# Router products of two tiles at once: 256 columns in odd steps of an attention loop, their sums over chunks in even steps

## The chip, the cores and the metric

The kernel runs on one core of one Trainium2 chip. The metric is the device time of one execution in microseconds. The trace comes from one profiled execution, whose times count from its first instruction.

## The reference

Attention within chunks of 64 rows is followed by a mixture of experts with one expert per token, all in fp32. In short:

```python
# q, k, v: (8, 8, 576, 64); chunks of 64 along the sequence
scores = q_c @ k_c.T / 8
attn = softmax(scores)
x = (attn @ v_c) -> (4608, 512)          # tokens x (heads * head_dim)

g_logits = x @ w_group                   # 4 groups
g_idx, g_w = argmax, its softmax weight
e_logits = x @ w_expert[g_idx]           # 4 experts of the group
e_idx, e_w = argmax, its softmax weight
y = relu(x @ w1[g, e]) @ w2[g, e]        # 512 -> 1024 -> 512
out = g_w * e_w * y
```

The router is the two products of x with w_group and with all four w_expert, 4 + 16 = 20 columns in all.

## The kernel before

**Tiles and stages.** The 4608 tokens are 36 tiles of 128, and 4 tiles make a routing group (groups 0 to 8). A tile passes through stages that a loop runs in steps, each stage on another tile, so that a step t works on up to six tiles. The order of the instructions of TensorE, VectorE and ScalarE is the order of the program, written out by hand (the `run` strings of the loop at L659 to L673, EXTRA, and TAIL for what comes behind). Step t issues:

- `b(t+1)`, stage_b, L294: scores of a tile, 16 small matmuls of 64x64 array tiles, into `scb[(t+1) % 2]`, a pair of PSUM banks. The scores fill columns 0 to 255 of either bank.
- `n(t-3)`, stage_norm, L339: VectorE takes the denominators (L343), their reciprocals (L345), one tile's row positions (L530, for the scatter of x to HBM on GpSimd's queue), and multiplies (L354) into x.
- `s(t)`, stage_sub, L304: VectorE takes the row maximum (L308) and subtracts it (L312).
- `c(t-1)`, stage_ct, L320: TensorE transposes the probabilities (L324), ScalarE copies them out of PSUM (L326).
- `tile_e(t)`, L378, from step 4 to step 32: the router, below.
- `p(t-2)`, stage_pv, L329: probabilities times values (L336), into the one pair of banks `ob`.
- four steps of routing (`more(4)`) on VectorE, then `e(t)`, the exponential on ScalarE (L318).
- `x(t-3)`, stage_xt, L359: TensorE transposes x (L366), ScalarE copies it to `xT` (L367), which holds the four tiles of a group.
- loads of q, k and v on SyncE's queue, and every fourth step `stage_e3` (L474), which ranks a group's tokens.

**The router.** The 512 channels of x are four chunks of 128. With tau = t - 4, `tile_e` multiplies tile tau by the 20 router columns (padded to 32) chunk by chunk: four matmuls (L387), each with a 128x32 weight `wg[:, c]` and 128 columns of `xT`, each in its own 32 columns of the array, so that they stand side by side on 128 partitions of PSUM, one chunk under the other. These are not summed in PSUM. The sum over the chunks, which also turns tokens onto partitions, is a matmul of its own (L391): the copied products of the tile before, 128x128, are its weights, and the constant `C_SEL`, 128x20, adds the four chunks. One copy of ScalarE (L392) brings both out of PSUM, 148 columns: the products of tile tau and the logits of tile tau - 1, into a slot of `lt8`. Both lie in columns 256 to 403 of the second bank of `scb[(t+1) % 2]`. After the logits of a group's last tile, at t = 4g + 8, `tile_e` queues `route(g)` (L412), whose steps VectorE takes whenever `more` is called: maximum (L421), comparison (L426), difference (L428), the first index (L432), then the softmax weights.

The last two groups, 7 and 8, don't go through `tile_e`: `stage_e1` (L369) multiplies a whole group's 512 columns at once and `stage_e2` (L398) sums its four tiles with four matmuls, in TAIL.

**Instructions.** One fp32 matmul of the program stands in the trace as two weight loads (PEld) and two matmuls (PE), the transposes as one of each. A step's scores, for instance, are 32 and 32.

**Beside the loop.** In steps 24 to 31 the first expert is prepared: GpSimd loads its weights, ScalarE casts them (L217), GpSimd subtracts (L218). Behind the loop and TAIL comes the expert part (from L731), two thirds of the time, which the change doesn't touch.

Of the kernel before, what the change touches and what calls it, by code (L numbers as in the profile page):

```python
# [9 lines left out]
F32 = mybir.dt.float32  # L10
# [9 lines left out]
P = 128  # L20
B, H, SEQ, HD = 8, 8, 576, 64
CH = 64
# [7 lines left out]
NG = 4  # L30
RPE = N // P
NG0 = NT // NG
GL = NG0 - 1
# [20 lines left out]
for _n in range(3 * NV, 3 * B):  # L54
# [3 lines left out]
C_ID, C_TRI, C_SEL, C_BASE, C_IOTA4, C_TID, C_T17, C_I64, C_J128, C_FORCE, C_BE, C_PBASE, C_E, C_PM, C_I16, C_PJ, C_PQ, C_PMIN, C_PNEED, C_N = (  # L58
    0, 128, 256, 276, 292, 296, 332, 349, 413, 449, 450, 451, 452, 453, 455, 471, 473, 475, 476, 477)
# [54 lines left out]
def moe_kernel(tc, qk, v, wgs, w1, w2, cst, out):  # L114
    nc = tc.nc
    w1 = w1.rearrange("g e d f -> (g e) d f")
    w2 = w2.rearrange("g e f d -> (g e) f d")
    with ExitStack() as ctx:
# [5 lines left out]
        cs = wpool.tile([P, C_N], F32, name="cs")  # L124
# [95 lines left out]
        with ExitStack() as c1:  # L220
            cpool = c1.enter_context(tc.tile_pool(name="cp", bufs=1))
# [7 lines left out]
            scb = [ps_s.tile([P, 2, 512], F32, name="sc%d" % i) for i in range(2)]  # L229
# [3 lines left out]
            def bank():  # L233

                ring.append(ring.pop(0))
                return ring[-1]
# [16 lines left out]
            wg = cpool.tile([P, 4, 32], F32, name="wg")  # L253
# [5 lines left out]

            xbufs = [cpool.tile([P, NG, XW], F32, name="x%d" % i) for i in range(3)]  # L260

            lt8 = cpool.tile([P, 2 * NG, P + 20], F32, name="lt8")

            st, TL = {}, NT - 1

# [103 lines left out]
            def stage_e1(g):  # L369
                xT = st["xT", g]  # L370
                lt = bank()
                for c in range(4):
                    nc.tensor.matmul(lt[32 * c:32 * c + 32, :], lhsT=wg[:, c, :], rhs=xT[:, c, :], start=True, stop=True)
                lts = lt8.rearrange("p a b -> p (a b)")[:, 0:512]
                nc.scalar.copy(lts, lt)
                st["lts", g] = lts

            def tile_e(t):  # L378

                n = (GL - 1) * NG  # L380
                e = scb[(t + 1) % 2][:, 1, 4 * CH:4 * CH + P + 20]
                t -= 4
                lo, hi = (0 if t < n else P), (P + 20 if t else P)
                if lo == 0:
                    g, i = divmod(t, NG)
                    for c in range(4):
                        nc.tensor.matmul(e[32 * c:32 * c + 32, 0:P], lhsT=wg[:, c, :], rhs=st["xT", g][:, c, i * P:i * P + P],  # L387
                                         start=True, stop=True)
                t -= 1
                if t >= 0:  # L390
                    nc.tensor.matmul(e[:, P:P + 20], lhsT=lt8[:, (t - 1) % 8, 0:P], rhs=cs[:, C_SEL:C_SEL + 20], start=True, stop=True)  # L391
                nc.scalar.copy(lt8[:, t % 8, lo:hi], e[:, lo:hi])  # L392
                if last(t):
                    g = t // NG
                    st["lg", g] = lt8[:, g % 2 * NG:g % 2 * NG + NG, P:P + 20]
                    routing.append(route(g))

            def stage_e2(g):  # L398
                lts = st["lts", g]
# [208 lines left out]
            routing = []  # L608
# [19 lines left out]
            def last(t):  # L628
                return t >= 0 and t % NG == NG - 1
# [8 lines left out]
            def run(seq):  # L638
                g = dict(u=warm_up, P=prep_static, X=first_x, L=first_l1, H=first_hi, D=first_lo, W=prep2_hi, w=prep2_lo, y=lambda i: prep2_lo(i, nc.vector), F=first_loads, R=reload, V=load_v,
                         Q=load_qk, q=load_first, I=load_cs, G=load_wg, C=casts, B=banks, Z=prefill)  # L640
                f = dict(b=stage_b, s=stage_sub, c=stage_ct, e=stage_exp, p=stage_pv, n=stage_norm, x=stage_xt)
                for z in seq.split():
                    if z[0] == "m":
                        more(int(z[1:]))
                    elif z[0] in g:
                        g[z[0]](int(z[1:]))
                    elif z[0] == "1":
                        stage_e1(int(z[1:]))
                    elif z[0] == "2":
                        stage_e2(int(z[1:]))  # L650
                    elif z[0] == "3":
                        stage_e3(int(z[1:]))
                    elif 0 <= int(z[1:]) < NT:
                        f[z[0]](int(z[1:]))

            with tc.manual_schedule(engines={mybir.EngineType.PE, mybir.EngineType.DVE, mybir.EngineType.Activation}):
                run(HEAD)
                run("u8 b0 u6")
                for t in range(TL - 2):  # L659
                    run("b%d n%d s%d c%d" % (t + 1, t - 3, t, t - 1) if t > 2 else ("b1 s0", "c0 b2 s1", "p0 b3 s2 c1")[t])  # L660
                    if 4 <= t <= 4 + (GL - 1) * NG:
                        tile_e(t)
                    run("p%d" % (t - 2) if t > 2 else "")
                    more(4)
                    run("e%d" % t)
                    stage_ex()
                    if t % 2 and t // 2 + NQ < NT // 2:
                        run("Q%d" % (t // 2 + NQ))
                    run("x%d" % (t - 3))
                    run(" ".join("V%d" % n for n in VS.get(t, ())))  # L670
                    if last(t - 7):
                        run("3%d" % ((t - 7) // NG))
                    run(EXTRA.get(t, ""))  # L673
                run(TAIL)
                assert not waiting
# [11 lines left out]
        def ft(n, name):  # L687

            at[0] += n
            return w2r[1].rearrange("p a b -> p (a b)")[0:E1, at[0] - n:at[0]]  # L690

        col = lambda c, n=1: cs[0:E1, c:c + n]
        co, a, na, s4, thr, end = ft(2, "co"), ft(RPE, "a"), ft(2, "na"), ft(4, "s4"), ft(1, "thr"), ft(1, "end")
# [732 lines left out]
```

## Time and profile before

| | us |
|---|---|
| three timed runs | 622.61, 632.97, 638.04 |
| their median | 632.97 |
| the profiled execution | 624.93 |
| its span, first to last instruction | 623.3 |
| mean granted TensorE clock of the span | 0.975 |

The page of the profile gives each engine's busy time and the share of the span. The chain of waits is the work that ended last, followed back from the end. The timeline merges instructions of one line that follow one another; "x8" is their number, and a bracket is the time for which the engine sat idle ahead of them, with what ended it ("issue" is nothing that the profile shows). [...] PE is TensorE's matmuls, PEld its weight loads, DVE is VectorE, ACT ScalarE, POOL GpSimd.

### The profile page before, as it was taken

What the parts mean: (1) busy time and instruction counts of PE and PEld (TensorE: products, weight loads), DVE (VectorE), ACT (ScalarE), POOL (GpSimd) and SP (SyncE); (2) the same over time, 40 slices, a digit from 0 to 9 for tenths busy, and PEclk for the clock granted to TensorE, in tenths of its full rate; (3) what the DMA queues carried; (4) which work ended last, traced back from release to release, by engine and by line L of the source; (5) the groups of instructions that cost most, each with busy time, mean ns of one, the idle gap of its engine ahead of it and who ended that gap; (6) DMA issues with size and microseconds to landing.
All of it is one profiled execution on the core that took longest, in us unless ns stands there. A gap on an engine that the chain in (4) does not pass through costs nothing.

```text
span 623.3 us, 16433 instructions
## 1 busy us (share of the span) xinstructions
PE 585.0 (94%) x5823; PEld 504.8 (81%) x5824; DVE 366.4 (59%) x688; ACT 264.9 (43%) x368; POOL 152.9 (25%) x279
## 2 busy tenths in 40 slices
PE   6889899966799999989999999999999999999995
PEld 3667677754789899878889899989989988898984
DVE  4577769885678682127497674735425578854311
ACT  2455556644246361016476362625215365552111
POOL 0003225573333211221332212221111111311120
PEclk9999989978989999989999999999999999999998
DMA  8999987673439883215489855452712778932110
GB/s 305 422 404 339 279 260 252 235 222 153 136 126 358 294 322 130 68 30 206 141 297 342 299 192 184 164 200 70 290 51 77 251 274 269 316 109 67 34 37 30
DMA packets 43106, 128.28 MB, mean 206 GB/s; under 512 B 4590, under 2 KB 4974, under 8 KB 41136
## 3 DMA queue, kind: packets, MB, share of 16 engines
q1 hardware_dynamic: 32192, 93.93, 43.5%
q0 software_dynamic: 10864, 33.64, 14.9%
q8 instruction: 36, 0.59, 0.4%
q14 instruction: 14, 0.11, 0.0%
HBM read 106.40 MB, written 21.93 MB: 206 GB/s over the span
## 4 chain that ended last, share of the span: by engine, by line
PE 85%; issue 5%; DVE 4%; DMA 2%; ACT 1%; SPq 1%; POOL 1%; DVEq 0%; ACTq 0%; POOLq 0%
PE py L872 29%; PE ph L857 20%; PE lgk L857 6%; PE ph L841 5%; PE o L336 3%; PE sc L300 3%; PE py L889 2%; PE pxt L757 2%; PE lgk L366 2%; PE tp L324 1%; DMA qk<-in_qk_dram 1%; PE sc L387 1%; PE sc L391 1%; PE ph L803 1%; PE py L826 1%
## 5 line engine op out<-in xcount | busy, mean ns | idle before, releaser
L857 PE MATMUL ph<-xt,w1h 128*128 128x256 f32 x672 | 100.1, 285 | 1.9 <-issue 1.9
L857 PEld LDWEIGHTS ph<-xt,w1h 128*128 128x128 f32 x672 | 90.6, 194 | 3.3 <-issue 2.3
L1013 ACT ACTIVATE hth<-ph 128x512 fp32r<-128x512 f32 x43 | 25.7, 598 | 154.4 <-PE ph L857 123.0
L1340 POOL DMA_INDIRECT out_dram<-xl,io__2891 x37 | 39.1, 1058 | 159.1 <-DVE xl L1076 143.7
L1090 DVE TENSOR_TENSOR w2l<-w2r,w2h 128x1024 fp32r<-128x1024 f32 x60 | 69.5, 1220 | 2.8 <-ACT w2h L1004 2.8
L1086 DVE TENSOR_TENSOR w1l<-w1r,w1h 128x2048 fp32r<-128x2048 f32 x28 | 63.1, 2288 | 13.2 <-ACT w1h L1000 11.0
L872 PE MATMUL py<-w2h,hth 128*128 128x512 f32 x264 | 67.6, 398 | 0.0
L872 PE MATMUL py<-w2l,hth 128*128 128x512 f32 x264 | 65.3, 390 | 0.0
L872 PE MATMUL py<-w2h,htl 128*128 128x512 f32 x264 | 65.2, 389 | 0.0
L1076 DVE TENSOR_SCALAR xl<-py,io__2891 128x512 f32<-128x512 f32 x33 | 24.8, 750 | 67.4 <-PE py L872 66.9
L1109 DVE SCALAR_TENSOR_TENSOR htl<-ph,hth 128x512 fp32r<-128x512 f32 x40 | 27.5, 688 | 59.6 <-ACT hth L1013 57.0
L872 PEld LDWEIGHTS py<-w2l,hth 128*128 128x128 f32 x264 | 49.6, 188 | 10.6
L872 PEld LDWEIGHTS py<-w2h,htl 128*128 128x128 f32 x264 | 49.6, 188 | 10.3
L872 PEld LDWEIGHTS py<-w2h,hth 128*128 128x128 f32 x264 | 47.6, 188 | 10.2 <-ACT hth L1061 0.9
L857 PE MATMUL ph<-xt,w1l 128*128 128x256 f32 x336 | 54.7, 285 | 0.5 <-DVE w1l L1086 0.5
L1000 ACT CAST w1h<-w1r 128x2048 fp32r<-128x2048 f32 x28 | 52.2, 1901 | 4.1 <-DMA w1r<-in_moe_w_dram 2.3
L1004 ACT CAST w2h<-w2r 128x2048 fp32r<-128x2048 f32 x28 | 52.4, 1923 | 1.3 <-DMA w2r<-in_moe_w_dram 1.3
L857 PEld LDWEIGHTS ph<-xt,w1l 128*128 128x128 f32 x336 | 46.8, 194 | 0.7 <-DVE w1l L1086 0.7
L300 PE MATMUL sc<-qk 64*64 64x64 f32 x1152 | 28.2, 233 | 8.5 <-issue 4.4
L519 POOL DMA_INDIRECT xs<-x,pos x24 | 24.3, 1014 | 46.1 <-DVE x L354 15.2
L300 PEld LDWEIGHTS sc<-qk 64*64 64x64 f32 x1152 | 22.3, 141 | 16.1 <-issue 5.9
L336 PE MATMUL o<-va,pT 64*64 64x65 f32 x1120 | 27.2, 232 | 8.4 <-issue 4.2
(285 smaller groups left out, 952.2 us busy)
## 6 DMA issues: line engine op xcount, KB each, us to landing
w1r<-in_moe_w_dram SPq DMA_DIRECT2D x30, 1024.0 KB, 7.0
w2r<-in_moe_w_dram SPq DMA_DIRECT2D x30, 1024.0 KB
qk<-in_qk_dram SPq DMA_DIRECT2D x15, 1024.0 KB
xgr<-xs POOLq DMA_DIRECT2D x38, 257.0 KB, 5.2
va<-in_v_dram SPq DMA_DIRECT2D x24, 390.0 KB
qk<-in_qk_dram SPq DMA_DIRECT2D x6, 512.0 KB
w1r<-in_moe_w_dram POOLq DMA_DIRECT2D x2, 1024.0 KB
w2r<-in_moe_w_dram POOLq DMA_DIRECT2D x2, 1024.0 KB
```

The source lines that it names most:

```text
L300: nc.tensor.matmul(sc[cols, x, hp * CH:hp * CH + CH], lhsT=T[rows, 0, hp, cols], rhs=T[rows, 1, hp, cols], start=True, stop=True)
L336: nc.tensor.matmul(o[cols, x, hp * W:hp * W + W], lhsT=pT[rows, hp, cols], rhs=v_at(2 * t + c)[rows, hp], start=True, stop=True)
L841: m = pe.matmul(ph[n], a_[:, c, 0:P], w_[:, c, n * 512:(n + 1) * 512], start=(i == 0), stop=(i == 11))
L857: m = pe.matmul(ph[f // 2][:, f % 2 * 256:f % 2 * 256 + 256], w_[:, c, f * P:(f + 1) * P], a_[:, c, :], start=(i == 0), stop=(i == 11))
L872: m = pe.matmul(py[j], a_[:, f, half[j]], w_(b, f), start=(i == 0), stop=(i == 23))
L1000: lambda b, s, j: ac.copy(wt[b][0][:, s], w1r[j]), K1)
L1004: lambda b, s, j: ac.copy(wt[b][2 + j], w2r[j]), K2)
L1013: ac.activation(hth()[:, 2 * b:2 * b + 2, :], ph[b].rearrange("p (f t) -> p f t", f=2), AF.Relu).then_inc(S["Ha"], 1)
L1086: lambda b, s, j: ve.tensor_sub(wt[b][1][:, s], w1r[j], wt[b][0][:, s].bitcast(F32)), K1, js)
L1090: m = ve.tensor_sub(wt[b][4 + 2 * j + i], w2r[j][:, 2 * i:2 * i + 2], wt[b][2 + j][:, 2 * i:2 * i + 2].bitcast(F32))
L1109: ve.scalar_tensor_tensor(out=htl()[:, 2 * b:2 * b + 2, :], in0=ph[b].rearrange("p (f t) -> p f t", f=2), scalar=0.0, in1=hth()[:, 2 * b:2 ...
L1340: gp.indirect_dma_start(out, bass.IndirectOffsetOnAxis(ap=io[:, j, 0:1].bitcast(I32), axis=0), yb[:, j, :], None, bounds_check=N - 1, oob_ ...
```

## The change

In odd steps (t odd, so tau odd) `tile_e` makes the products of tiles tau - 1 and tau together, four matmuls of 256 columns, and ScalarE copies 256 columns to `lt4`, a buffer of four tiles. In even steps from t = 6 on it makes the sums of the two tiles whose products the step before made, two matmuls of 20 columns, and ScalarE copies 40 columns to `lg8`. Step 4 has nothing any more; step 32 has two sums. The even steps use the first bank of the pair instead of the second. `stage_e1` copies its products of a group to `lt4`.

```diff
-            lt8 = cpool.tile([P, 2 * NG, P + 20], F32, name="lt8")
+            lt4 = cpool.tile([P, NG, P], F32, name="lt4")
+            lg8 = cpool.tile([P, 2 * NG, 20], F32, name="lg8")
...
-                lts = lt8.rearrange("p a b -> p (a b)")[:, 0:512]
+                lts = lt4.rearrange("p a b -> p (a b)")
...
-                n = (GL - 1) * NG
-                e = scb[(t + 1) % 2][:, 1, 4 * CH:4 * CH + P + 20]
+                sc = scb[(t + 1) % 2]
                 t -= 4
-                lo, hi = (0 if t < n else P), (P + 20 if t else P)
-                if lo == 0:
-                    g, i = divmod(t, NG)
+                if t % 2:
+                    g, i = divmod(t - 1, NG)
+                    e = sc[:, 1, 4 * CH:4 * CH + 2 * P]
                     for c in range(4):
-                        nc.tensor.matmul(e[32 * c:32 * c + 32, 0:P], lhsT=wg[:, c, :], rhs=st["xT", g][:, c, i * P:i * P + P],
+                        nc.tensor.matmul(e[32 * c:32 * c + 32, :], lhsT=wg[:, c, :], rhs=st["xT", g][:, c, i * P:i * P + 2 * P],
                                          start=True, stop=True)
-                t -= 1
-                if t >= 0:
-                    nc.tensor.matmul(e[:, P:P + 20], lhsT=lt8[:, (t - 1) % 8, 0:P], rhs=cs[:, C_SEL:C_SEL + 20], start=True, stop=True)
-                nc.scalar.copy(lt8[:, t % 8, lo:hi], e[:, lo:hi])
-                if last(t):
-                    g = t // NG
-                    st["lg", g] = lt8[:, g % 2 * NG:g % 2 * NG + NG, P:P + 20]
-                    routing.append(route(g))
+                    nc.scalar.copy(lt4[:, i:i + 2].rearrange("p a b -> p (a b)"), e)
+                elif t:
+                    t -= 2
+                    e = sc[:, 0, 4 * CH:4 * CH + 40]
+                    for i in range(2):
+                        nc.tensor.matmul(e[:, 20 * i:20 * i + 20], lhsT=lt4[:, (t + i) % NG], rhs=cs[:, C_SEL:C_SEL + 20], start=True, stop=True)
+                    nc.scalar.copy(lg8[:, t % 8:t % 8 + 2].rearrange("p a b -> p (a b)"), e)
+                    if last(t + 1):
+                        g = t // NG
+                        st["lg", g] = lg8[:, g % 2 * NG:g % 2 * NG + NG]
+                        routing.append(route(g))
```

## Rows read from the trace of the kernel before

**Rows 1.** The page: busy time by engine, and the chain's shares by engine

```profile
PE 585.0 (94%) x5823; PEld 504.8 (81%) x5824; DVE 366.4 (59%) x688; ACT 264.9 (43%) x368; POOL 152.9 (25%) x279
...
PE 85%; issue 5%; DVE 4%; DMA 2%; ACT 1%; SPq 1%; POOL 1%; DVEq 0%; ACTq 0%; POOLq 0%
```

**Rows 2.** TensorE's timeline, one step and the next one's start: start, busy us, line

```profile
85.71 0.69 PE L300 MATMUL sc<-qk 64*64 64x64 f32 x32
86.34 0.65 PE L324 MATMUL lgk<-cs,pr 128*128 128x128 f32 x4
86.92 0.42 PE L387 MATMUL sc<-xT,wg 128*32 128x128 f32 x8
87.28 0.40 PE L391 MATMUL sc<-cs,lt 128*128 128x20 f32 x2
87.61 0.70 PE L336 MATMUL o<-va,pT 64*64 64x65 f32 x32
88.23 0.66 PE L366 MATMUL tp<-cs,xl 128*128 128x128 f32 x4
88.82 0.69 PE L300 MATMUL sc<-qk 64*64 64x64 f32 x32
```

**Rows 3.** Who waited, weight loads, 14 to 160 us: total us, times, longest

```profile
PEld sc L391 <- issue: 5.5, 27, 0.4
PEld sc L387 <- issue: 4.2, 24, 0.3
```

**Rows 4.** TensorE's timeline behind the loop: a group's products, transposes, four sums, values

```profile
141.96 1.06 PE L373 MATMUL sc<-xT,wg 128*32 128x512 f32 x8 [0.72 <-DVE pr L312]
143.72 0.66 PE L366 MATMUL sc<-cs,xl 128*128 128x128 f32 x4 [0.70 <-ACT lt L375]
144.22 0.97 PE L402 MATMUL lgk<-cs,lt 128*128 128x20 f32 x8
145.11 0.70 PE L336 MATMUL sc<-va,pT 64*64 64x65 f32 x32
```

**Rows 5.** ScalarE's groups by shape, 19 to 130 us: busy us, mean ns, idle before

```profile
L318 ACT ACTIVATE pr<-pr 128x512 f32<-128x512 f32 x29 | 18.4, 633 | 7.9 <-DVE se L457 3.6 <-DVE pr L312 1.5 <-issue 0.9
...
L392 ACT COPY lt<-sc 128x148 f32<-128x148 f32 x27 | 7.6, 283 | 3.0 <-PE sc L391 1.7 <-issue 0.4
...
L392 ACT COPY lt<-sc 128x20 f32<-128x20 f32 x1 | 0.2, 186 | 0.0
```

**Rows 6.** Stretches cut at TensorE's starts behind its stops: length, then busy (number) by engine

```profile
22.58:28.66 6.08, 5.32 (x128) 4.01 (x127) 2.42 (x6) 3.38 (x7) 0.00 (x0) 1.00 1.03 427
28.66:34.69 6.03, 4.76 (x127) 3.69 (x128) 4.53 (x10) 2.57 (x5) 0.00 (x0) 1.00 1.00 413
34.69:40.78 6.09, 5.27 (x129) 3.96 (x128) 4.15 (x19) 3.61 (x8) 0.00 (x0) 1.00 1.03 405
...
64.47:75.66 11.19, 10.04 (x256) 7.63 (x256) 9.68 (x37) 6.20 (x13) 3.49 (x6) 1.00 0.87 262
```

**Rows 7.** The chain of waits in order of time: start, us, what

```profile
90.19 0.58 ACT pT L326
...
98.01 0.69 DVE pr L312
...
101.47 0.61 DVE pr L312
...
102.12 0.69 PE sc L300 x32
```

**Rows 8.** The stretch behind the last stop

```profile
75.66:83.12 7.46, 7.46 (x124) 5.73 (x125) 3.83 (x10) 2.57 (x5) 1.98 (x3) 0.57 0.94 264
```

**Rows 9.** Timelines of VectorE and of GpSimd near step 32

```profile
127.11 4.43 DVE L432 SCALAR_TENSOR_TENSOR one<-one,cs 128x80 f32<-128x80 f32 x1
...
127.74 3.70 POOL L218 TENSOR_TENSOR w1l<-w1r,w1h 128x512 fp32r<-128x512 f32 x3
```

**Rows 10.** Who waited, 30 to 220 us: VectorE's first routing step

```profile
DVE mx L421 <- ACT lt L392: 6.2, 6, 1.8
```

## The prediction

> **What bounds the kernel now.** I read the page first: its busy shares and its chain of waits by engine. TensorE is busy 94% of 623.3 us and carries 85% of the chain that ended last; VectorE, the next, is busy 59% [rows 1]. The change lies in the attention loop alone, so the second view is TensorE's timeline of one attention step there. A step of 3.11 us from one stage_b to the next (85.71 to 88.82 us) has six pieces, one behind the other: scores 0.63, transposes of the probabilities 0.58, the router's four products 0.36 (eight instructions, since each fp32 matmul stands as two), its sum over chunks 0.33, values 0.62, transposes of the output 0.59 [rows 2]. I count each piece from its start to the next one's start. The router is thus 0.69 of 3.11 us, and nothing but TensorE's own queue stands between the pieces.
>
> Third, who waited: the weight load of the products sat idle 4.2 us in 24 waits and that of the sum 5.5 us in 27, both put down to issue, no other engine [rows 3]. That is 0.17 and 0.20 us per step between one kind of array use (128x128) and another (128x32). Fourth, the steps that are not 3.11 us, of which there are three kinds, priced below: waits for instructions before 76 us [rows 6], a stretch at half clock [rows 8], and steps in which VectorE is late [rows 7].
>
> **The change part by part.** Before, every step from t = 4 to 32 has products (the last none) and a sum (the first none). Afterwards odd steps have four products of 256 columns and no sum, even steps two sums and no products; step 4 has neither.
>
> *Odd step.* Eight instructions of 128 columns are busy 0.42 us; eight of 512 columns are busy 1.06 us [rows 2, 4]. That is 0.64 us for 384 columns, so 128 more columns cost 0.21 us, and the products take 0.36 + 0.21 = 0.57 us. The sum's 0.33 us is gone. Saved: 0.69 - 0.57 = 0.12 us.
>
> *Even step.* In the tail eight sum instructions follow four transposes directly: 143.72 to 145.11 us, 1.39 us from the transposes to the values, and the eight alone 0.89 us, 0.11 each [rows 4]. With four of them it is 1.39 - 0.45 = 0.94 us. Today the same distance, transposes to values, is 86.34 to 87.61, 1.27 us [rows 2]. Saved: 0.33 us. The second sum is cheap because there is no longer a 128x32 piece between it and the transposes.
>
> A pair of steps saves 0.45 us of TensorE, a step 0.225 us on average. Step 4 loses its products, 0.36 us. Step 32 gets a second sum, +0.2 us, but it lies behind ScalarE's casts and counts nothing. All of it, 28 steps, would be 0.4 + 27 x 0.225 = 6.4 us. That is the upper end of the plain sum; the lower end is zero, if another engine holds every step.
>
> *ScalarE.* One copy of 148 columns takes 283 ns, one of 20 columns 186 ns [rows 5], 0.76 ns a column. So 256 columns are 365 ns and 40 columns 201 ns: 566 ns a pair, as much as 2 x 283. I take nothing. In odd steps the copy ends 0.08 us later; behind it waits the exponential, which in rows of this loop waits for VectorE anyway, so 0.08 us is its price if that cover goes. In even steps, where a group's routing starts, the sums end sooner and the copy is shorter. VectorE waited 6.2 us in six groups for that copy [rows 10], and may get 0.1 to 0.2 us of each back: 0 to 1.2 us in all, taken as nothing because ScalarE's copy of the probabilities stands ahead of it in the queue.
>
> *What is issued elsewhere.* No DMA, no queue and no routing step moves: group g's logits are complete at step 4g + 8 as before, and the step's loads and scatters stand where they stood. No new wait is added; the sums read what ScalarE copied a step earlier, the products what it copied at the end of the step before, as today.
>
> *Where the saving reaches the end.* I go through the loop by stretches.
>
> Up to 53 us TensorE stops after every 256 of its instructions. Stretches cut at the starts behind the stops hold about 128 matmuls and as many weight loads each, and last 6.08, 6.03 and 6.09 us, although the work in them is 5.32, 4.76 and 5.27 us [rows 6]. The stop takes up what the work leaves over: the instructions come every 6.1 us whatever is done with them. So in this stretch I count instructions, not work. A step has 82 matmuls and 82 loads; afterwards 80 and 76, a mean of 78 and 78, 4.9% fewer. Of the 34 us from 19 to 53 that is 1.7 us, and step 4's 16 instructions at 6.08/256 us are another 0.4. I take 2.0 us. If the stop were a fixed cost per block, eight steps x 0.225 + 0.36 = 2.2 us: nearly the same, so this choice matters little.
>
> [...]
>
> From 53 to 75.7 us the stop comes after every second block: 11.19 us with work of 10.04 [rows 6]. By instructions 4.9% of 22.5 us is 1.1 us, by work six steps x 0.225 = 1.35. I take 1.1.
>
> From 75.7 to 92 us no stop is left; five steps would give 1.1 us. At 90.19 the chain of waits goes over to ScalarE [rows 7], so the last of them is left out: 0.9.
>
> From 92 to 126 us VectorE is often late. Its chain runs without a pause from the subtraction at 98.01 to the one at 101.47, after which TensorE's scores start at 102.12 [rows 7]. A step of TensorE shortened here is a longer wait. I give three of nine steps, 0.4 us rather than the 2.0 that nine would be. If VectorE had room, 1.6 us more.
>
> Behind step 32 the code is the same, and its chain hangs on the loop's end; it moves forward whole.
>
> Sum: 2.0 + 1.1 + 0.9 + 0.4 = 4.4 us, 0.7%. The profiled execution took 624.93 us (span 623.3), so it would take 620.5. The three timed runs are 622.61, 632.97 and 638.04, median 632.97, 8 us above the profiled one. Of the four executions the middle two average 628.95; I set the forecast against that: 624.5 us.
>
> *What stays unknown.* On one step VectorE's L432 took 4.43 us, while GpSimd's three subtractions of the first expert's weights ran for 3.70 us [rows 9]. If the phase shifts so that VectorE passes ahead, some 4 us go; if another instruction is caught by others of these subtractions, as much is added. I take zero, since both engines hang on the same casts; both ends are in the range.
>
> **The rivals.**
>
> *A: hidden.* VectorE or ScalarE takes up nearly all. For it: the unbroken VectorE chain [rows 7]; its work per step is near TensorE's. Against it: up to 76 us TensorE's stops give VectorE slack. The gain is then the early stretch, 1.5 us or less: profiled execution 623.4, forecast 627.5.
>
> *B: more.* The instruction stops thin out and the stretch at half clock from 75.66 to 83.12 does not come, since the stop of 11.19 - 10.04 = 1.15 us ahead of it is gone. [...] 6.4 + 1.1 + 3 = 10.5 us: profiled 614.4, forecast 618.5. [...]
>
> *C: slower, by the clock.* Where instructions set the pace, less work in a block means longer stops: 256 instructions are 1.64 steps of 2.89 us, 4.7 us of work in 6.08, so 1.3 us of idle instead of 0.9. One stop of 1.15 us was already followed by half clock, though those before 53 us, up to 1.27, were not. [...] It decides from the second one on: -4.4 + 6 = +1.6 us, profiled 626.5, forecast 630.5. Against it: granted clock 1.00 in all stretches before 75.66 [rows 6].
>
> **How the numbers follow.** Forecast 0.62, A 0.20, B 0.09, C 0.09. The predicted time is 624.5 us. The runs of before lie 15.4 us apart, 2.4%, so a median of a few runs can miss by half of that; 2% is about what a measurement of this kernel can tell from no change. The range takes A's, B's and C's times and the 4 us of VectorE's stall: 617 to 634 us. None of the cases alone reaches 2% (12.5 us): faster by more needs B and the stall's 4 us, or a lucky draw of runs, 0.12; slower by more needs three further stretches at half clock or an unlucky one, 0.04; within 2% 0.84.
>
> **What would show it.** Right: on TensorE's timeline odd steps with products of about 0.57 us and no sum, even steps with four sum instructions and 0.94 us from transposes to values; a plain pair of steps of 5.8 us instead of 6.2; blocks up to 53 us that still last about 6.1 us, with longer stops; step 32 reached some 4 us sooner. Wrong: blocks that last clearly longer or shorter than 6.1 us; products of 256 columns at over 0.7 us; more waits of the values for VectorE's L354 before 76 us; a granted clock of half in a stretch that had none.

## The result, and the profile after

Over 19 runs of each kernel the changed one took 620.02 us in the median (613.16 to 625.63), the kernel before 625.91 (620.93 to 638.04). The ratio is 0.9904, with a 95% interval of 0.9878 to 0.993: 1% faster, 4 to 8 us. The forecast was 624.5 us in a range of 617 to 634, 4.4 us below the centre of before.

A ratio leaves out the slow executions, those more than 1.5% above the fastest of their kernel, here 7 of the changed kernel's 19 (622.99 to 625.63 us); by the medians of all 19 it is 0.9906.

Two further comparisons, each against before on the same chip, make that less certain. One gave 0.9898 [0.9816, 0.998], but on three of seven runs; the mean of all seven is 623.62 us beside 623.61 of before. The other gave 0.999 [0.9954, 1.0026] on 12 runs. The gain lies between nothing and 1%, and why it varies is the main thing that the experiments show.

| profiled execution | before | after |
|---|---|---|
| time, us | 624.93 | 621.86 |
| span, us | 623.3 | 620.2 |
| mean granted TensorE clock | 0.975 | 0.969 |
| scores of step 4, start | 14.6 | 13.4 |
| scores of step 24, start | 92.6 | 89.2 |
| scores of step 33, start | 123.6 | 122.4 |
| first products of group 8 (the tail) | 154.8 | 150.6 |
| first product of the expert part | 189.6 | 185.6 |

Here and below a step is named by the tile whose scores open it: "step 33" is step 32 of the program, which starts with the scores of tile 33.

The changed page, as [rows 1]: 112 matmuls fewer, 3.1 us less of TensorE, and a chain with the same shares.

```profile
PE 581.9 (94%) x5711; PEld 503.1 (81%) x5712; DVE 365.8 (59%) x688; ACT 263.5 (42%) x367; POOL 154.2 (25%) x279
...
PE 85%; issue 5%; DVE 4%; DMA 3%; ACT 1%; POOL 1%; SPq 1%; DVEq 0%; ACTq 0%; POOLq 0%
```

TensorE's timeline of an even step (with the ranking of a group in it) and an odd one, as [rows 2]:

```profile
57.09 0.66 PE L325 MATMUL lgk<-cs,pr 128*128 128x128 f32 x4
57.58 0.52 PE L394 MATMUL sc<-cs,lt 128*128 128x20 f32 x4
58.03 0.70 PE L337 MATMUL o<-va,pT 64*64 64x65 f32 x32
...
59.85 0.69 PE L301 MATMUL sc<-qk 64*64 64x64 f32 x32
60.47 0.66 PE L325 MATMUL tp<-cs,pr 128*128 128x128 f32 x4
61.06 0.64 PE L387 MATMUL sc<-xT,wg 128*32 128x256 f32 x8
61.63 0.70 PE L337 MATMUL o<-va,pT 64*64 64x65 f32 x32
62.26 0.66 PE L367 MATMUL lgk<-cs,x 128*128 128x128 f32 x4
62.84 0.29 PE L301 MATMUL sc<-qk 64*64 64x64 f32 x4
```

The products of 256 columns take 61.06 to 61.63, 0.57 us. In the even step transposes to values is 57.09 to 58.03, 0.94. The odd step is 2.99 us, and an even one without the ranking 0.62 + 0.94 + 0.63 + 0.59 = 2.78: a plain pair of 5.77 us.

ScalarE's two copies by shape, as [rows 5], and VectorE's first routing step in the list of who waited, as [rows 10], where 6.2 us in six waits became 2.6 in three:

```profile
L389 ACT COPY lt<-sc 128x256 f32<-128x256 f32 x14 | 5.2, 373 | 0.9 <-PE sc L387 0.8
...
L395 ACT COPY lg<-sc 128x40 f32<-128x40 f32 x14 | 2.8, 197 | 0.7 <-PE sc L394 0.7
...
DVE mx L424 <- ACT lg L395: 2.6, 3, 0.9
```

Stretches cut at TensorE's starts behind its stops, with the columns of [rows 6]: the length, busy time and number of PE, PEld, DVE, ACT and POOL, then the granted clock (1.00 is the whole clock, 0.50 half of it), the share of the DMA engines and GB/s. The last line is one around a low clock:

```profile
21.73:27.86 6.13, 5.00 (x128) 3.88 (x129) 3.14 (x7) 3.34 (x7) 0.00 (x0) 1.00 1.03 424
27.86:40.09 12.23, 11.54 (x255) 8.41 (x256) 9.44 (x33) 6.74 (x14) 0.00 (x0) 0.86 1.02 412
40.09:46.11 6.02, 5.48 (x128) 4.25 (x127) 4.33 (x9) 3.24 (x7) 0.00 (x0) 1.00 1.03 382
46.11:52.35 6.24, 4.54 (x128) 3.83 (x127) 5.47 (x20) 2.70 (x7) 2.35 (x4) 1.00 1.03 401
52.35:65.08 12.73, 12.01 (x255) 8.89 (x255) 8.60 (x27) 6.49 (x13) 3.67 (x7) 0.87 0.96 355
65.08:75.70 10.62, 10.08 (x255) 7.65 (x256) 8.96 (x34) 6.78 (x15) 3.50 (x6) 1.00 0.87 248
75.70:81.59 5.89, 4.49 (x127) 3.84 (x127) 5.12 (x19) 2.70 (x7) 1.93 (x3) 1.00 1.00 359
...
107.40:114.90 7.50, 7.50 (x125) 5.95 (x125) 6.54 (x18) 4.25 (x9) 4.87 (x6) 0.54 0.77 266
```

Up to 52 us blocks of 256 instructions still last 6.0 to 6.2 us, and the idle time in one is now up to 6.24 - 4.54 = 1.70 us. After that longest stop the stretch from 52.35 has a clock of 0.87, with 0.55 from 52.7 to 56.5: TensorE ran at about half clock there. The half-clock stretch of before, 75.66 to 83.12 [rows 8], is gone (1.00 from 75.70). In its place stand stretches at about 15 to 19, 29 to 33, 53 to 56 and 107 to 115 us, with clocks of 0.64, 0.55, 0.55 and 0.54, the last for 7.50 us. That last one follows a stop of 1.64 us, with which the chain of waits quoted here ends:

```profile
89.68 0.68 DVE x L355
90.36 0.59 DVE m L309
...
99.86 0.69 DVE x L355
...
103.77 0.57 PE sc L387 x8
104.33 0.28 PE o L337 x8
104.61 1.64 issue
```

From 89.68 to 100.55 the chain runs through VectorE, as between 90 and 102 us before [rows 7]. Last, VectorE's stall, from timelines of both engines as in [rows 9]:

```profile
129.57 4.21 DVE L470 TENSOR_TENSOR cum<-cum 128x16 bf16<-128x16 bf16 x1
130.04 3.70 POOL L218 TENSOR_TENSOR w1l<-w1r,w1h 128x512 fp32r<-128x512 f32 x3
...
134.67 0.96 PE L337 MATMUL o<-va,pT 64*64 64x65 f32 x32 [4.43 <-DVE x L355]
```

It has nearly the same length (4.43 us before), on another instruction.

### The profile page after: what moved, and what is told of

The parts are those of the page before. It is cut to its first block, busy times and chain, and to the rows that moved or that the text cites. A ratio compares the mean times of both kernels' runs of the same rounds, so it can differ in the third digit from the quotient of the medians.

```text
span 620.2 us, 16208 instructions
## 1 busy us (share of the span) xinstructions
PE 581.9 (94%) x5711; PEld 503.1 (81%) x5712; DVE 365.8 (59%) x688; ACT 263.5 (42%) x367; POOL 154.2 (25%) x279
## 4 chain that ended last, share of the span: by engine, by line
PE 85%; issue 5%; DVE 4%; DMA 3%; ACT 1%; POOL 1%; SPq 1%; DVEq 0%; ACTq 0%; POOLq 0%
PE py L875 29%; PE ph L860 20%; PE lgk L860 7%; PE ph L844 5%; PE o L337 3%; PE sc L301 3%; PE py L892 2%; PE pxt L760 2%; PE lgk L367 2%; PE tp L325 1%; DMA qk<-in_qk_dram 1%; PE lgk L325 1%; PE tp L367 1%; PE sc L387 1%; PE ph L806 1%
## 5 line engine op out<-in xcount | busy, mean ns | idle before, releaser
L1089 DVE TENSOR_TENSOR w1l<-w1r,w1h 128x2048 fp32r<-128x2048 f32 x28 | 63.0, 2289 | 13.1 <-ACT w1h L1003 11.1
L337 PEld LDWEIGHTS o<-va,pT 64*64 64x64 f32 x1120 | 22.5, 147 | 19.4 <-issue 7.3
```

Source lines behind the costliest of these rows:

```text
L337: nc.tensor.matmul(o[cols, x, hp * W:hp * W + W], lhsT=pT[rows, hp, cols], rhs=v_at(2 * t + c)[rows, hp], start=True, stop=True)
L1089: lambda b, s, j: ve.tensor_sub(wt[b][1][:, s], w1r[j], wt[b][0][:, s].bitcast(F32)), K1, js)
```

## The experiments

Theory 1 is the prediction's: where DMA traffic is high (a share of 1.00 to 1.03 in the 6 us blocks of [rows 6]), TensorE is paced by its instructions, so that fewer of them save time and less work alone does not. From e9 on it takes in rival C's half: idle time in a block can be followed by half clock, as the 1.70 us above were. The rival, theory 2, says that the work taken out is what counts.

One trace is one execution, so the table stands beside all of them. The second column is the time from the scores' start of step 4 to that of step 24, the fourth from there to the expert part's first product. The third is the granted clock from 14 to 90 us.

| kernel | steps 4 to 24, us | clock | to expert part, us | ratio to before |
|---|---|---|---|---|
| before | 78.0 | 0.96 | 97.0 | 1 |
| after | 75.8 | 0.93 | 96.4 | 0.9904 |
| after again (e5) | 80.4 | 0.87 | 97.8 | 0.9898 |
| after again (e11) | 80.6 | 0.90 | 98.2 | 0.999 |
| sums paired only (e1, e8) | 83.8, 77.1 | 0.90, 0.93 | 99.3, 92.7 | 1.003, 1.001 |
| before, wide products (e2) | 80.4 | 0.96 | 99.1 | 0.9975 |
| piece before sums (e3) | 80.5 | 0.89 | 98.8 | 1.0147 |
| loads later (e4) | 79.9 | 0.91 | 99.2 | 0.9967 |
| products split (e6) | 84.7 | 0.91 | 96.4 | 1.0078 |
| four tiles at once (e7) | 77.6 | 0.93 | 97.8 | 0.9983 |
| after, wide scores (e9) | 74.2 | 0.97 | 98.3 | 0.9982 |
| four tiles, wide scores (e10) | 72.4 | 0.98 | 98.9 | 1.0034 |
| after, subtractions spread (e12) | 78.7 | 0.91 | 94.7 | 0.9951 |

**Work without instructions, on the kernel before (e2).** Every step's products are 256 columns wide, the second 128 a copy that nobody reads: 0.21 us more work a step, 5.9 us in all.

```diff
-  nc.tensor.matmul(e[32 * c:32 * c + 32, 0:P], lhsT=wg[:, c, :], rhs=st["xT", g][:, c, i * P:i * P + P],
+  nc.tensor.matmul(ew[32 * c:32 * c + 32, :], lhsT=wg[:, c, :],
+                   rhs=st["xT", g][:, c, i * P:i * P + P].unsqueeze(1).broadcast_to([P, 2, P]),
```

> The kernel before with products of 256 columns in every step (the tile's own 128 twice, the second half unused): 0.21 us more work on TensorE in each of 28 steps and not one instruction more. Theory 1 (up to about 53 us TensorE's instructions come at 256 per 6.1 us whatever the work): the stops before 53 us shrink by about 0.3 us each, blocks of 256 instructions still last 6.0 to 6.2 us there, and only the later steps pay: 2 to 4 us more than before. Theory 2 (a stop is a fixed cost per block, all of TensorE's work counts): the stops stay at 0.8 to 1.3 us, blocks last about 6.4 us, 5.9 us more than before.

Measured: 0.9975 [0.9938, 1.0011]. Over the runs the added work cost nothing, so that theory 1's 2 to 4 us for the later steps were missed as well as theory 2's 5.9. In the stretches view, cut at its stops, blocks last 6.02 to 6.90 us, and the idle time in one, 0.65 to 1.44 us from 29.31 to 48.57, is 0.36 us in the next:

```profile
29.31:35.33 6.02, 4.97 (x128) 3.68 (x128) 4.31 (x10) 2.76 (x6) 0.00 (x0) 1.00 1.00 412
35.33:41.67 6.34, 5.69 (x128) 3.96 (x127) 4.40 (x19) 3.64 (x8) 0.00 (x0) 1.00 1.03 404
41.67:48.57 6.90, 5.46 (x128) 4.06 (x127) 5.13 (x14) 2.61 (x6) 0.00 (x0) 1.00 1.03 392
48.57:54.59 6.02, 5.66 (x127) 3.93 (x128) 2.86 (x9) 3.38 (x7) 1.33 (x2) 1.00 0.89 354
54.59:76.57 21.98, 21.25 (x510) 15.35 (x510) 18.59 (x69) 12.49 (x26) 7.01 (x12) 1.00 0.89 290
```

The mean clock of its runs was 0.975, that of before on the same chip 0.964, so part of the work may have been paid by the clock: drawn through each kernel's own runs, at a clock of 0.97, e2 stands at 629.0 us and before at 627.8.

**The same on the changed kernel (e9), with a control (e11).** Half of the scores' matmuls write 128 columns; the second 64 are overwritten or not read. A step's scores rise from 0.63 to 0.84 us.

```diff
-  nc.tensor.matmul(sc[cols, x, hp * CH:hp * CH + CH], lhsT=T[rows, 0, hp, cols], rhs=T[rows, 1, hp, cols], ...)
+  k = T[rows, 1, hp, cols]
+  if hp % 2:
+      nc.tensor.matmul(sc[cols, x, hp * CH:hp * CH + 2 * CH], lhsT=T[rows, 0, hp, cols],
+                       rhs=k.unsqueeze(1).broadcast_to([CH, 2, CH]), start=True, stop=True)
+  else:
+      ...
```

> The changed kernel, in which the scores' matmuls of every second head pair write 128 columns instead of 64: their own 64 columns of k twice, the second copy overwritten or unread. No instruction more; by the price of 128 further columns (0.21 us for eight instructions) about 0.2 us more work on TensorE in each of some 35 steps, 6 to 7 us. Theory 1 (where DMA traffic is high, TensorE is paced by its instructions; work that is taken out of a block there becomes idle time, and a longer stop is followed by half clock): the work fills the stops; the time stays within 2 us of the changed kernel's, or goes below it, with a higher mean granted clock and shorter stops. Rival (the work counts, and the changed kernel's gain is its saved work): 4 to 7 us slower than the changed kernel, that is, slower than before or level with it.

> The changed kernel again, as the control for the others of this call: 0.985 to 1.000 of before. If the gain depends on the granted clock of an execution, its single times lie in the same spread as the kernel before's, and at equal clock some 2 to 5 us below.

Measured: 0.9982 [0.9953, 1.0011] with the work, 0.999 [0.9954, 1.0026] without; medians 625.28 and 628.22. Some 7 us more work cost nothing in the time, as theory 1 had it; on the same line at a clock of 0.97 they cost 1.0 us (627.3 beside 626.3). The stretch from 14 to 90 us of before, the control and e9, in that order:

```profile
14.00:90.00 76.00, 66.38 (x1603) 50.79 (x1603) 52.61 (x170) 38.56 (x80) 13.00 (x29) 0.96 0.97 349
```

```profile
14.00:90.00 76.00, 64.93 (x1489) 49.46 (x1489) 51.78 (x165) 37.15 (x78) 13.05 (x29) 0.90 0.93 349
```

```profile
14.00:90.00 76.00, 69.08 (x1613) 52.69 (x1610) 55.95 (x177) 40.23 (x84) 14.17 (x31) 0.97 0.96 359
```

The control finished 1489 matmuls in these 76 us, e9 1613, though each of its steps holds more work. TensorE's idle time falls from 76 - 64.93 = 11.1 to 6.9 us, and the clock is 0.97 instead of 0.90. The control shows where the rest went: in its timeline of TensorE stops of 1.72 and 1.25 us follow one another, and the stretch behind them has a clock of 0.77.

```profile
54.24 0.34 PE L301 MATMUL sc<-qk 64*64 64x64 f32 x5 [1.72 <-issue]
...
60.95 0.37 PE L367 MATMUL tp<-cs,x 128*128 128x128 f32 x1 [1.25 <-issue]
```

```profile
60.00:75.00 15.00, 13.86 (x283) 10.20 (x282) 9.10 (x35) 6.64 (x14) 3.49 (x6) 0.77 0.69 218
```

**The changed kernel again (e5).**

> The changed kernel unaltered, on the chip of the runs beside it, so that these can be compared with it. Both theories: 4 to 7 us less than before (ratio 0.988 to 0.994).

Measured: three runs of 615.38 to 619.77 us with mean clocks of 0.976 to 0.983, four of 627.13 to 630.07 with 0.955 to 0.963. Within the kernels timed here 0.01 of mean clock went with 1.4 to 7 us, some 4 us as a rule. Drawn through each kernel's own runs, at a clock of 0.97, the changed kernel stands at 622.8 us where before stands at 624.9 (this chip), and at 626.3 against 626.7 (the chip of e11): 2.1 and 0.4 us better at equal clock. That line is a fit over few runs, an indication and no proof.

**The instructions put back (e6).** The products of two tiles still stand in one step, as eight matmuls of 128 columns.

```diff
-  for c in range(4):
-      nc.tensor.matmul(e[32 * c:32 * c + 32, :], ..., rhs=st["xT", g][:, c, i * P:i * P + 2 * P], ...)
+  for j in range(2):
+      for c in range(4):
+          nc.tensor.matmul(e[32 * c:32 * c + 32, j * P:j * P + P], ..., rhs=st["xT", g][:, c, (i + j) * P:(i + j) * P + P], ...)
```

> The changed kernel with its products of 256 columns as two matmuls of 128 columns each in the same odd steps: 16 TensorE instructions more in every odd step, so that the number of instructions is again that of the kernel before, with about 0.06 us more work a pair of steps. Theory 1 (up to 75 us the number of instructions sets the pace, 256 per 5.5 to 6.1 us): 2 to 4 us more than the changed kernel, half of the gain or more is lost. Theory 2 (TensorE's work and the missing turns of the array make the gain): at most 1 us more than the changed kernel.

Measured: 1.0078 [1.0039, 1.0116]; its mean is 626.55 us, that of e5 on the same chip 623.62, so 2.9 us come back. Theory 1 expects 2 to 4, the rival at most 1, but with e5's seven runs so far apart the 95% interval of that difference is about -2 to 8 us, and the medians (626.50 and 627.13) differ the other way. What the runs do show is that its ratio lies above all three of the changed kernel, of which the highest reaches up to 1.0026. Its size, and with it the choice between the theories, stays open here. Part may be clock again: in its trace stops of 1.45 to 2.18 us follow one another up to 70 us, and the granted clock is 0.83 from 40 to 60 us.

**Fewer instructions still (e7, e10).** Products of four tiles in one step, four sums in the next: 32 instructions per four steps instead of the changed kernel's 48. e10 adds the wide scores of e9.

```diff
+  if last(t):
+      stage_e1(t // NG)
+  elif t and t % NG == 0:
+      ...
+      for i in range(NG):
+          nc.tensor.matmul(e[:, 20 * i:20 * i + 20], lhsT=lts[:, i * P:(i + 1) * P], ...)
```

> The router's products of a whole group, 512 columns, in the last step of a group and the sums of its four tiles in the step behind it; the two other steps have neither. Instructions of the router per four steps: 32 instead of the change's 48 and the 80 of before. Its work, by what stands on the timelines so far: products 0.99 instead of 2 x 0.57 us, sums 0.81 instead of 2 x 0.36, so nearly the same, and one turn of the array fewer. Theory 1 (instructions set the pace up to 75 us): 1.5 to 2.5 us less than the changed kernel. Theory 2 (work): within 0.7 us of it. If the longer copy of 512 columns or the third bank in a step makes TensorE wait, more.

> The router's products of four tiles at once (512 columns) and four sums in the next step, 32 instructions per four steps instead of 48 in the changed kernel, together with the wide scores of the run before. Four tiles at once alone came out 0.2% from before, with stops of up to 2.4 us and half clock behind them. Theory 1: the added work shortens those stops, the half clock behind them goes, and the saving of instructions shows: 2 to 5 us faster than four tiles at once without the added work, level with the changed kernel or 1 to 2 us below it. Rival (four tiles at once lost by the placement of its 512 columns and its sums): with 6 us more work it is slower by 4 to 7 us.

Measured: 0.9983 [0.9942, 1.0024] and 1.0034 [1.0001, 1.0068]. Both miss theory 1's numbers. e7's trace has stops of 2.12, 1.14 and 2.37 us before 42 us, and behind the last of them a clock of 0.66:

```profile
40.00:50.00 10.00, 8.56 (x129) 5.51 (x129) 3.95 (x9) 2.98 (x6) 0.00 (x0) 0.66 1.03 392
```

In e10 three stops over 0.5 us are left up to 100 us (1.26 to 1.63), the clock from 14 to 90 us is 0.98, and steps 4 to 24 are the shortest of all: 72.4 us, 1.8 below e9. With 16 instructions fewer per four steps at 6.1/256 us each, 20 steps should save 1.9. So in that one execution the instructions count as theory 1 has it, up to step 24. From there to step 33 it took 32.9 us, e9 30.9, and the gain was gone. Over its runs e10 was slower than e9 all the same, by 3 us; what of the four-tile form costs that is open.

**The sums alone (e1, e8).** Products every step as before, two sums every second step. e1 had a wait that I had not planned: the sums stood behind ScalarE's copy of the products made in the same step.

```diff
-  nc.tensor.matmul(e[:, P:P + 20], lhsT=lt8[:, (t - 1) % 8, 0:P], rhs=cs[:, C_SEL:C_SEL + 20], ...)
+  if t % 2 == 0 and t:
+      for i in range(2):
+          nc.tensor.matmul(e[:, 20 * i:20 * i + 20], lhsT=lt4[:, (t + i) % NG], rhs=cs[:, C_SEL:C_SEL + 20], ...)
```

> The sums of two tiles stand together in even steps as in the change, but the products stay at one tile, 128 columns, in every step. Theory 1 (the pairing of the products and the missing 128x32 piece in even steps make the gain): the distance from the transposes of the probabilities to the values is 0.94 us in odd steps (no sum) and about 1.5 us in even steps (products, then four sum instructions), 2.43 a pair against 2.54 before and 2.05 after; the number of TensorE instructions is that of before; so 0.7 to 1.5 us less than before. Rival (bringing the sums together is what counts, or steps of unequal length): 4 us less than before or more.

Who waited, TensorE in e1 from 14 to 130 us:

```profile
PE sc L394 <- ACT lt L389: 6.0, 10, 0.8
```

1.003 [0.9999, 1.0062] thus holds 6 us of a wait that isn't the change's, and decides nothing. e8 issues that copy behind the sums instead:

> The first experiment again, with ScalarE's copy of the step's products behind the two sums in the program, so that the sums don't wait for it (there TensorE sat idle 0.5 us ahead of the sums in every even step). Products of 128 columns in every step, two sums in even steps; as many instructions as before; 2.43 us from transposes to values a pair of steps against 2.54 before. Theory 1 (instructions up to 75 us, work behind it): within 1 us of the kernel before, that is 4 to 6 us more than the changed kernel. Rival (sums brought together are the gain): within 2 us of the changed kernel.

Measured: 1.001 [0.9976, 1.0044]. The sums' half alone is worth nothing that can be measured. That the change's gain needs the wide products as well is likely beside 0.9904 and 0.9898 and not shown: over all runs on this chip e8 has a mean of 622.88 us and the changed kernel (e5) one of 623.62.

**A 128x32 piece before the sums (e3).** One matmul of one column with a router weight, its result unread, between the transposes and the sums of each even step: does the sum cost more behind another kind of array use, as [rows 3] suggest?

```diff
+  nc.tensor.matmul(sc[0:32, 0, 4 * CH + 64:4 * CH + 65], lhsT=wg[:, 0, :], rhs=cs[:, C_SEL:C_SEL + 1], start=True, stop=True)
```

> The changed kernel with one more matmul of a 128x32 weight and one column, into unused PSUM columns, ahead of the two sums in even steps: two loads and two matmuls with next to no array work. Theory 1 (going from 128x128 to 128x32 and back costs 0.17 and 0.20 us, which the even steps had been spared): the distance from transposes to values in even steps goes from 0.94 to about 1.25 us; 2 to 4.5 us more than the changed kernel. Rival (the piece costs only its own short instructions): 1.0 us in even steps, 1 us more or less in all.

```profile
83.98 0.65 PE L325 MATMUL lgk<-cs,pr 128*128 128x128 f32 x4
84.57 0.22 PE L393 MATMUL sc<-cs,wg 128*32 128x1 f32 x2
84.72 0.62 PE L395 MATMUL sc<-cs,lt 128*128 128x20 f32 x4
85.27 0.70 PE L337 MATMUL o<-va,pT 64*64 64x65 f32 x32
```

Transposes to values: 83.98 to 85.27, 1.29 us instead of 0.94, for two instructions of one column. The piece costs 0.35 us, where the prediction had 0.17 and 0.20 for the two changes of array use. The time, though, is 1.47% [1.1, 1.84] above before, 9 us, and 11 us above e4, a form of the changed kernel on the same chip, where 14 x 0.35 is 4.9. In its trace 7 us more lie in the expert part, which is the same code (441.7 us beside 434.6 after): TensorE's waits between 190 and 300 us were

```profile
PE ph L861 <- issue: 9.0, 3, 5.1
```

and in the changed kernel

```profile
PE ph L860 <- issue: 2.7, 2, 1.8
```

Fifty-six more instructions ahead of the expert part may have moved which of its instructions meet a stop. That is argued and not shown: in the twelve other traces, with other counts ahead of it, such waits of over 0.4 us in the expert part sum to 1.7 to 3.2 us.

**Loads two pairs later (e4).** The changed kernel with less loaded ahead, so that DMA traffic has gaps.

```diff
-HEAD = "... Q4 V4 Q5 V5 Q6"
+HEAD = "... Q4 V4 V5"
...
-  if t % 2 and t // 2 + NQ < NT // 2:
-      run("Q%d" % (t // 2 + NQ))
+  if t % 2 and t // 2 + NQ - 2 < NT // 2:
+      run("Q%d" % (t // 2 + NQ - 2))
```

> The changed kernel with the loads of q and k issued two pairs of tiles later (five pairs ahead instead of seven), so that 2 MB less are under way early. Theory 1 (a block of instructions is late because its packet stands behind loads on busy DMA engines): the DMA share falls below 1.0 some 5 us sooner, the stops of TensorE end sooner, and the time is 1 to 3 us less than the changed kernel's. Theory 2 (the stop is a fixed cost per block): same stops, same time within 1 us. If the loads come too late, TensorE's scores wait for q and k and the time is more.

```profile
17.28:23.41 6.13, 4.20 (x127) 3.35 (x127) 4.81 (x11) 2.28 (x4) 1.21 (x9) 1.00 1.01 414
23.41:29.54 6.13, 4.99 (x127) 3.87 (x127) 2.35 (x5) 3.34 (x7) 0.00 (x0) 1.00 1.01 420
42.62:55.00 12.38, 12.38 (x204) 9.93 (x207) 5.10 (x13) 3.97 (x8) 1.19 (x2) 0.59 0.57 204
```

With the DMA engines full (1.01) a block takes 6.13 us, whether 4.20 or 4.99 us of it is work. With them at 0.57 TensorE runs 12.38 us without a stop, but at a clock of 0.59, right behind one of 1.85 us; at that clock its 411 instructions took 12.38 us, 7.7 for 256, so this stretch decides nothing on DMA. All traces together say more. From 14 to 125 us and at full clock, 117 crossings of a block lie behind 6 us with a DMA share over 0.95, and 81 of them have a stop of 0.5 us or more; 38 lie behind a share under 0.7, and none has. The time, 0.9967 [0.9935, 0.9999], doesn't separate it from the changed kernel.

**VectorE's stall (e12).** Two of the last three casts and subtractions of the first expert move from the end of the loop's step 31 into the program's steps 33 and 34.

```diff
-  31: "P4 P5 P6"}
-TAIL = ("b34 n30 s33 c32 m1 p31 m2 e33 x30 b35 n31 s34 m1 c33 P7 ...
+  31: "P4"}
+TAIL = ("b34 n30 s33 c32 m1 P5 p31 m2 e33 x30 b35 n31 s34 m1 P6 c33 P7 ...
```

> The changed kernel with two of GpSimd's three last steps of the first expert's preparation (casts on ScalarE and subtractions on GpSimd) moved from step 31 to behind steps 33 and 34, so that the subtractions no longer run as one block beside VectorE's routing. It prices the 4.2 us stall of VectorE that the changed kernel has on L470 as the kernel before had it on L432. If the stall is on the path: 2 to 4 us faster than the changed kernel. If it is covered, or moves to another VectorE instruction beside another subtraction: within 1 us.

Measured: 0.9951 [0.9918, 0.9983], median 623.35 beside 628.22 of the control e11. The point estimates differ by 0.4%, 2.4 us, and the intervals overlap, since both hang on the same runs of before. Compared with each other, the means of the runs that the ratios use (623.74 and 626.98) are 3.2 us apart, with a 95% interval of about 1.3 to 5.2: e12 is faster. That it is so for want of the stall is not shown, for the control's own trace has no stall: its three subtractions, 134.39 to 138.13, met these instructions of VectorE, all at their usual length.

```profile
133.59 0.69 DVE L355 TENSOR_TENSOR x<-o,rc 128x512 f32<-128x512 f32 x1
134.20 0.68 DVE L309 TENSOR_REDUCE m<-sc 128x8 f32<-128x512 f32 x1
134.92 0.69 DVE L313 TENSOR_TENSOR pr<-sc,m 128x512 f32<-128x512 f32 x1
```

So the same three subtractions, in the same kernel, ran once beside a stall (after, 4.21 us) and once without; what decides it isn't shown. In the two traces e12 is 4.2 us shorter from step 33 to the expert part (62.6 beside 66.8), with no stall in the longer one. So what the stall costs in the time stays open.

## Why the prediction came out as it did

**The prices of the pieces were right.** 0.57 us for the wide products, 0.94 from transposes to values and 5.77 us for a plain pair stand in the changed timeline as worked out, because they came from rows of the same operations in the tail [rows 4]. The reason given for the cheap second sum agrees with e3: put a 128x32 piece back and the even step takes 1.29. ScalarE's copies, 373 and 197 ns, are within 8 ns of the straight line through [rows 5].

**Blocks that keep their length: right.** They last 6.0 to 6.2 us after the change too, with stops of up to 1.70 us, and e2, e9 and e4 look at it from three sides: with work added to the kernel before, two of e2's four blocks from 29.31 us on at 6.02 us (the others 6.34 and 6.90); with work added to the changed kernel, 6.04 us per 256 instructions over the 76 us of e9 (1613 + 1610 of them); and 4.20 and 4.99 us of work in equal blocks of 6.13 us in e4. For what TensorE waits in a stop the views have no name but "issue". From 20 to 80 us the DMA queues of before moved ten packets of the kind "instruction", beside 4327 of queue q1:

```profile
q1 hardware_dynamic: 4327, 19.12, 88.5%
...
q8 instruction: 10, 0.16, 1.1%
```

That a stop is a wait for one of these is my reading, which no run shows. What the traces show is idle time of 0.5 us or more at 81 of 117 crossings behind a DMA share over 0.95; the longest stop quoted here is 2.37 us (e7).

**The step that failed is the sum along the loop.** It put 4.0 us (2.0 + 1.1 + 0.9) before 92 us and 0.4 behind. In the traces steps 4 to 24 gained 78.0 - 75.8 = 2.2 us, steps 24 to 33 lost them (31.0 before, 33.2 after), and from 4 to 33 both kernels took 109.0 us. So the sign that the prediction names, step 32 reached some 4 us sooner, did not come: it was 1.2 us (123.6 and 122.4). The span's 3.1 us come from elsewhere: 1.2 from ahead of step 4, where TensorE waits for the loads of q and k (1.6 us in before), which the change doesn't touch; 0.6 + 2.4 from step 33 to group 8's products; and from there to the end 0.2 + 0.9 were lost. The 2.4 us are for the most part one wait of the kernel before, which the changed kernel's timeline does not have:

```profile
151.54 0.99 PE L366 MATMUL sc<-cs,xl 128*128 128x128 f32 x4 [2.18 <-DVE xl L354]
```

So the agreement of 4.4 us with the measured 4 to 8 isn't that of its terms; as far as the profiled pair shows, it is luck. What the sum lacked is the clock. It counted the saved instructions at the pace of a full-clock execution and left what follows a longer stop to a rival. An estimate from the granted clocks, which takes TensorE as busy wherever the clock was low: from step 4 to 24 the time lost to the clock (the stretch times what its clock lacks to 1.00) was 78.0 x 0.044 = 3.4 us before (clock 0.956) and 75.8 x 0.068 = 5.1 after (0.932), from 24 to 33 nothing before and 33.2 x 0.103 = 3.4 after (0.897). Without that time the change gains 3.9 us up to step 24, where the sum had 4.0, and 1.1 behind, where it had 0.4. By this estimate the saving was there, and 8.5 us lost to half clock instead of 3.4 took it back. No run shows the 3 us that rivals B and C put on a stretch at half clock; in its place this estimate gives 3.4 us for the one of before, and in the changed kernel 5.1 for three up to step 24 and 3.4 for the fourth.

**Rival C's half clock came, though the time wasn't C's.** Lower clocks followed longer stops: 0.87 from 52.35 to 65.08 behind 1.70 us, 0.54 from 107.4 to 114.9 behind 1.64, 0.77 from 60 to 75 in the control behind 1.25. A granted clock of half in a stretch that had none was one of the prediction's signs of being wrong, and it came. That stops up to 1.27 us (1.49 by the timeline) had passed without it before held only for that execution: after, the stretch from 27.86, behind a stop of 1.13, has 0.86. No length decided it alone. Over all traces from 14 to 125 us, 23 of 31 stops of 1.6 us or more were followed by half clock within 3.5 us, and 9 of 38 stops of 1.0 to 1.6. The counts give the order of the two; that the stop is the cause isn't shown. Rival B's half came too: the stretch at 75.66 to 83.12, 0.57 before, went (1.00 from 75.70 to 88.06). The balance of the two differs from execution to execution, which fits that the same kernel gave 0.990 and 0.999.

**Rival A's stretch: as forecast, with a worse end.** VectorE's chain from 89.68 to 100.55 let nothing more be gained: the lead over before was 3.4 us at step 24 (89.19 against 92.63) and 3.5 at step 28 (102.41 against 105.93). It did not take the lead away. That did the stop of 1.64 us and the clock of 0.54 behind it, which left 0.4 us at step 30 (112.05 against 112.48). e10, first at step 24 of all kernels, lost its lead over e9 in the same steps, at a granted clock of 1.00; why is open.

**The stall: right to leave at zero.** It moved from L432 to L470 at the same 4.2 to 4.4 us. Both of these have two SBUF inputs; they took 4.43 and 4.21 us and ended within 0.1 us of the last subtraction, while in the control L470 took 0.17 and the instructions that read PSUM beside the subtractions ran their 0.7. What holds VectorE there, the traces don't show, nor which engine came first: VectorE's recorded starts lie 0.63 and 0.47 us ahead of the first subtraction's. In e5's trace a third was caught for 4.20 us, L465, which has one tensor input, so that two inputs are not what it takes.

**The range** held every median of the changed kernel: 620.02, 627.13 and 628.22 us. Its width, set by the spread of before and by the rivals' half-clock stretches, was the part that the repeats bore out best.

## What to carry to other kernels

Where an engine stops after every so many instructions, as TensorE did here after 256 in 6.0 to 6.2 us up to 52 us, count instructions and not work there, and test it by adding work that costs no instruction: if time and clock stay, there is nothing to save in that work; if the clock rose, as in e2 (0.975 beside 0.964) and e9 (0.97 beside 0.90), some of the price may be hidden in it. Then ask what the freed time turns into, since a stop of TensorE of 1.6 us or more was followed by half clock 23 times of 31, which in the profiled pair, by the estimate above, gave back what the change had saved. A gain under 1% that hangs on the clock wants the control repeated on a second chip, with each run's clock beside its time, before it is believed.

## What was not expected

- More work can go with a shorter loop. e9 put 0.21 us into each step of the changed kernel and passed steps 4 to 24 in 74.2 us instead of 75.8 to 80.6, at a clock of 0.97 instead of 0.87 to 0.93.
- The stops fall at the same counts in every kernel. Counting the traces' matmuls and weight loads from the start, those over 0.5 us that no other engine explains stand, up to 100 us, at 443, 697, 951, 1206, 1460 and so on, 254 or 255 records apart and the same within one or two in before and in each experiment; some are missing, none is in between. So a change moves which instruction is hit, in code that it doesn't touch as well.
- The single profile is a weak judge here. Three traces of the same changed kernel passed steps 4 to 24 in 75.8, 80.4 and 80.6 us, as wide as the whole effect that was forecast.
